# Narrow warm-up matmuls and two moved units in a fused state-space and feed-forward kernel

## The chip, the cores and the metric

The kernel runs on one core of a Trainium2 chip. The metric is the device time of one execution in microseconds (us), as the median of several runs. The engines are named as in the profile: PE is TensorE (its weight loads are listed as PEld), DVE is VectorE, ACT is ScalarE, POOL is GpSimd, SP is SyncE, which here only issues transfers.

## The reference

Two computations follow each other. The first is a chunked state-space scan over x (4 x 8 x 768 x 32), with decays a and projections B and C of width 16; the second is a bilinear feed-forward layer over its 3072 x 256 result.

```python
for c in range(nc):                       # chunks of the sequence
    cum = np.cumsum(la, axis=-1)
    L = np.exp(cum[:, :, :, None] - cum[:, :, None, :]) * causal
    CB = np.einsum('bhin,bhjn->bhij', Cc, Bc)
    y_intra = np.einsum('bhij,bhjd->bhid', CB * L, xc)
    y_inter = np.einsum('bhin,bhnd->bhid', Cc, state) * np.exp(cum)[..., None]
    y[:, :, sl] = y_intra + y_inter
    ...                                   # state = decay * state + B (x) x
x = y.transpose(0, 2, 1, 3).reshape(B * S, H * D)
a = x @ w_a                               # 256 -> 1536
b = x @ w_b
out = (a * b) @ w_out                     # 1536 -> 256
```

Inputs and outputs are float32; inside, products are taken in float16 with float32 sums.

## The kernel before

The sequence is cut into 6 blocks of 128 tokens, and the 4 batch rows into 2 pairs, which gives 12 units of work called pairs (0 to 11; pair p belongs to block p // 2). For each pair the state-space part does the following. `scale_bc` multiplies B and C by decay factors (`bm`, `cm`); a turn (`transposes` on PE for pairs 0 to 3, a transposing transfer `turn` for the later ones) gives `BT` and `CT`; `scores` takes the products of the two into the four score banks `SC`; `mask` applies the causal mask, on DVE, or, with `by_pool`, by a copy on ACT (`tmp`) and a product on POOL; `pv` or `outputs` multiplies the masked scores with `X16`, the scaled x (`scale_x`, on ACT or POOL), and adds the state's part.

The feed-forward part takes pairs 0 to 3 one by one: `unit(p, k2)` multiplies a pair with two of the twelve column tiles of Wa (`aps`) and of Wb (`bps`), ACT copies the first product out (`asb`), DVE multiplies the two (`times`, L714). `out_half` multiplies with Wo (L729). From block 2 on whole blocks are taken (`bunit`, `bout`, L759 and L784). `go((p, k2), ...)` issues whole units.

Nothing plans the order: it is written out by hand, and each engine works its instructions in program order. The result banks of PE other than `SC` are four, and the string `BANKS` says for each request in turn which of the four it gets; a request waits until the bank's last reader is done.

The start is a warm-up of PE on a tile of zeros (`warmup(n, bank, cols)`, L255), with 26 matmuls of 128 columns, then the decay scan on DVE, the factor products on PE (`factors_mm`, L283), their reciprocal on DVE (`fB`), pair 0's and pair 1's scaling, turn, scores and masks, with further warm-ups in between, mostly of 512 columns. The weights come on POOL's queue in pieces: the first half of Wa, a quarter of Wb (`load_w0`), x of pair 1, then, behind the first mask on POOL, the second quarter of Wb and the second halves.

Two later stretches matter here. After pair 1's first units the kernel issues four Wa products in a row (`us`), then their four Wb products with the multiplications, then the turn of pair 2, units (1, 4) and (1, 5), a small product `gps` and the scores of pair 2. And around pairs 4 and 5 it issues units (3, 0) to (3, 2), the scores of pair 5 with its masks and the scaling of pair 4's x on POOL (`prep_x(4)`), `out_half(2, 1)`, units (3, 3) to (3, 5), and then `group(2)`, which takes pairs 4 and 5 through `outputs` (L579, L489, L517).

Of the kernel before, what the change touches and what calls it, by code (L numbers as in the profile page):

```python
# [10 lines left out]
f32 = mybir.dt.float32  # L11
# [8 lines left out]
YS = 16.0  # L20

BANKS = (
    "01232012301230123012301230123012032103213021302132013201320132013201302310231023120130213"
    "0213023120312031203123012301230123012301230123012031203120312031203120312031203120312031"
)


# [1 line left out]
def kernel(  # L29
# [48 lines left out]
    Wb = [  # L78
        [big.tile([128, 2, KC // 2], f16, name=f"Wb0{t}") for t in range(2)],
        big.tile([128, 2, KC], f16, name="Wb1"),  # L80
    ]
# [22 lines left out]
    ffh = ctx.enter_context(tc.tile_pool(name="ffh", bufs=4))  # L104
# [7 lines left out]
    SC = [SC0[:, 0], SC0[:, 1], SC1[:, 0], SC1[:, 1]]  # L112
# [9 lines left out]
    def bank(name):  # L122
        return psf.tile([128, 512], f32, name=name, tag=f"ff{next(banks)}")
# [54 lines left out]
    def w_of(W, k, f):  # L178
        t_, q3 = W[k // 6], k % 6 // 3
        cols = t_[q3][:, f] if isinstance(t_, list) else t_[:, f, q3 * 384 : (q3 + 1) * 384]  # L180
        return cols.rearrange("p (c kk) -> p kk c", kk=3)[:, k % 3]
# [71 lines left out]
    def warmup(n, bank, cols=512):  # L253
        for _ in range(n):
            nc.tensor.matmul(  # L255
                bank[:, 0:cols], warm[:, 0:128], warm[:, 0:cols], start=True, stop=True, skip_group_check=True
            )


    def scan(lo, hi):  # L260
        for k in range(lo, hi):
            nc.vector.tensor_tensor_scan(Pr[:, k], a_sb[:, k], zero, 1.0, ALU.mult, ALU.add)
# [12 lines left out]
    def factors_mm(lo, hi, fps=None, k0=0):  # L275
        if fps is None:
            fps = bank("fps")
        w = 2 * NBP * H
        F = fps[:, k0 * w : (k0 + hi - lo) * w].rearrange("p (k r c) -> p k r c", k=hi - lo, r=2)
        for k in range(lo, hi):  # L280
            for r in range(2):
                for bt in range(2):
                    nc.tensor.matmul(  # L283
                        F[64 * bt : 64 * bt + 64, k - lo, r],
                        Pr[:, k].rearrange("p (i r) -> p r i", r=2)[:, r],
                        selr[:, k, bt],
                        start=True,
                        stop=True,
                        skip_group_check=True,
                        tile_position=(0, 64 * bt),  # L290
                    )
        return F.rearrange("p k r c -> p (k r c)")
# [14 lines left out]
    def flat(f, lo, hi):  # L307
        return f[:, lo:hi].rearrange("p k r b h -> p (k r b h)")
# [13 lines left out]
    def scale_bc(p, which, eng, factor=None):  # L322
        blk, bp = divmod(p, NBP)
        name, f = (("bm", fB), ("cm", fC))[which]
        raw = by_token(pair_in[p][which]) if p >= P0 else pair_in[p][which].rearrange("p h r n -> p r h n")
        if p >= P0 and which:
            eng.tensor_tensor(
                out=planes[p % 2][:, 4:6].rearrange("p t (h n) -> p t h n", n=N),
                in0=raw,
                in1=of_pair(f, blk, bp).unsqueeze(3).broadcast_to((128, 2, H, N)),  # L330
                op=ALU.mult,
            )
            return
        m_ = mid.tile([128, 2, H, N], f16, name=name, tag=name)
        eng.tensor_tensor(  # L335
            out=m_,
            in0=raw,
            in1=(of_pair(f, blk, bp) if factor is None else factor).unsqueeze(3).broadcast_to((128, 2, H, N)),
            op=ALU.mult,
        )  # L340
        st.setdefault(p, {})[name] = m_
        if p >= P0:
            dst = planes[p % 2][:, 0:4].rearrange("p (t e) (m f n) -> p t e m f n", e=2, f=2, n=N)
            for e in range(2):
                eng.tensor_copy(dst[:, :, e, :, e], m_.rearrange("p t (m f) n -> p t m f n", f=2)[:, :, :, e])
# [76 lines left out]
    def scores(p):  # L422
        BT, CT = st[p]["BT"], st[p]["CT"]
        st[p]["T1"] = mid.tile([128, H, 2, Q], f16, name="t1", tag="t1")
        for e, bt, m in itertools.product(range(2), range(2), range(4)) if p >= P0 else ():
            rows = slice(32 * m, 32 * m + 32)
            c0 = (e * 2 + bt) * Q
            nc.tensor.matmul(  # L428
                SC[m][:, c0 : c0 + Q],
                BT[rows, e, bt],  # L430
                CT[rows, bt],
                start=True,
                stop=True,
                skip_group_check=True,
                tile_position=(32 * m, 0),
            )
        for e in range(2) if p < P0 else ():
            for r in range(2):
                for m in range(4):
                    for bt in range(2):  # L440
                        rows = slice(32 * m, 32 * m + 32)
                        c0 = (e * 2 + r) * Q
                        nc.tensor.matmul(  # L443
                            SC[m][64 * bt : 64 * bt + 64, c0 : c0 + Q],
                            BT[rows, e, r, bt],
                            CT[rows, bt],
                            start=True,
                            stop=True,
                            skip_group_check=True,
                            tile_position=(32 * m, 64 * bt),  # L450
                        )
# [13 lines left out]
    def product0(m2, e):  # L465

        return (
            st[0]["T1"][:, 4 * m2 : 4 * m2 + 4].rearrange("p (m e) r q -> p e m (r q)", e=2)[:, e],
            (SC0, SC1)[m2][:, :, e * 256 : e * 256 + 256],
        )  # L470
# [203 lines left out]
    def unit_mm(p, k2, W, kks=range(2), ps=None):  # L674
        if ps is None:
            ps = bank("aps" if W is Wa else "bps")
        for kk in kks:
            k = 2 * k2 + kk
            for f in range(2):
                nc.tensor.matmul(  # L680
                    ps[:, kk * 2 * Q : (kk + 1) * 2 * Q],
                    w_of(W, k, f),
                    X2T[:, p, :, f],
                    start=(f == 0),
                    stop=(f == 1),
                    skip_group_check=True,
                )
        return ps
# [14 lines left out]
        return [pss[k2] for k2 in ks]  # L703

    def evac_a(a_ps, on_dve=False):
        asb = ffh.tile([128, 512], f32, name="asb", tag="asb")
        (nc.vector.tensor_copy if on_dve else nc.scalar.copy)(asb, a_ps)  # L707
        return asb

    def times(p, k2, b_ps, asb):  # L710
        s = st[p]
        if "hk" not in s:
            s["hk"] = ffh.tile([128, NK, 2 * Q], f16, name="hk", tag="hk")
        nc.vector.tensor_tensor(  # L714
            out=s["hk"][:, 2 * k2 : 2 * k2 + 2, :].rearrange("p k q -> p (k q)"), in0=b_ps, in1=asb, op=ALU.mult
        )

    def unit(p, k2, between=None):
        a_ps = unit_mm(p, k2, Wa)
        if between:  # L720
            between()
        b_ps = unit_mm(p, k2, Wb)
        asb = evac_a(a_ps)
        return lambda: times(p, k2, b_ps, asb)
# [92 lines left out]
    def go(*items):  # L817
        for p, k2 in items:
            unit(p, k2)()
# [2 lines left out]
        if ("S", p) in st:  # L822
            st[p].update(st.pop(("S", p)))

    warmup(26, SC[3], 128)
    scan(0, 1)
    over_mid(0, 1)
    sel_over_mid(0, 1, nc.vector)
# [3 lines left out]
    fps = bank("fps")  # L832
    v = factors_mm(0, 1, fps)
    nc.vector.reciprocal(flat(fB, 0, 1), v)
    warmup(1, SC[3])
    v1 = factors_mm(1, 2, bank("fps"))
    warmup(1, SC[3])
    scale_bc(0, 0, nc.vector)
    scale_bc(0, 1, nc.vector, v.rearrange("p (r b h) -> p r b h", r=2, b=NBP)[:, :, 0])
    scan(3, 4)  # L840
    tb, tcp = bank("tb"), bank("tc")
# [1 line left out]
    nc.scalar.copy(flat(fC, 0, 1), v)  # L843
    nc.scalar.copy(flat(fC, 1, 2), v1)
    scan(4, 5)
    warmup(1, SC[3])
    warmup(2, SC[3], 128)
    scores(0)
    scale_bc(1, 0, nc.gpsimd)
    mask(product0(0, 0))  # L850
# [1 line left out]
    mask(product0(1, 1), by_pool=True)  # L852
    scale_bc(1, 1, nc.vector)
    mask(product0(1, 0))
    warmup(3, tcp)
    part = transposes1(0, bank("tb"))
    part(0)
    part(1)
    warmup(2, tcp)
    py = [bank("py0"), bank("py1")]  # L860
    pv_u(0, 0, py, True)
    ds_mm(0, 256, py)
    transposes1(1, SC[0])
    for bt in range(2):
        evac0(0, bt, nc.scalar, py)
    warmup(1, tcp)
    pv_u(0, 1, py, True)
    for bt in range(2):
        evac0(1, bt, nc.scalar, py)
# [18 lines left out]
    asb = [evac_a(aps[0])]  # L888
# [35 lines left out]
        load1(nc.sync, 3, 1, bt)  # L924
    loads_x(3, nc.sync)
    loads_bc(4)
    us = [(0, 3), (0, 4), (1, 3), (0, 5)]
    asb = [evac_a(unit_mm(p, k2, Wa)) for p, k2 in us]
    for (p, k2), a_ in zip(us, asb):
        times(p, k2, unit_mm(p, k2, Wb), a_)  # L930
    transposes(2, apart=True)
    go((1, 4))
    h = unit(1, 5)
    gps = bank("gps")
    for c0 in (0, 64):
# [115 lines left out]
    prep(6)  # L1051
    masked(4, (0, 1, 2))
    out_half(2, 0)
    go((3, 0), (3, 1), (3, 2))
    scores(5)
    mask(product(5, 3), by_pool=True, by_token=True)
    prep_x(4)
# [3 lines left out]
    loads_bc(8)  # L1061
    masked(5, (0, 1, 2))
    out_half(2, 1)
    go((3, 3), (3, 4))
    scale_x(5, nc.scalar)
    go((3, 5))
    group(2)
# [92 lines left out]
```

## Time and profile before

| | us |
|---|---|
| median of 3 runs | 121.4 |
| lowest and highest run | 121.36, 122.35 |
| profiled execution, its own time | 122.31 |
| its span, from the first to the last instruction | 120.6 |
| PE busy (matmuls) | 114.6 |
| DVE, ACT, POOL busy | 87.2, 72.7, 62.3 |

The span is the part that the profile divides; the remaining 1.7 us of the execution lie around it. Busy time is a mean over stages with different limits, so it has to be read stage by stage. Times of instructions are counted from the span's start. In the lists an instruction has its start, its duration, its engine, the kernel's line, the operation, the tiles written and read, and in brackets the idle time of the engine before it with what ended it; "issue" means that nothing which the profile shows was waited for.

### The profile page before, as it was taken

The numbers are of one execution on the slowest core, as the hardware profiler recorded it, in microseconds if no ns is written. First come the engines' busy times: TensorE is split into PE (matmuls) and PEld (weight loads), VectorE is DVE, ScalarE is ACT, GpSimd is POOL, SyncE is SP. The second block draws the span as 40 slices with busy tenths as digits, with TensorE's granted clock in tenths as the row PEclk, the third lists the DMA queues.
The fourth block names the chain that finished last, engine by engine and source line by source line (L and its number), as shares of the span: only waits on it lengthen the run. The fifth ranks groups of instructions, "written<-read, shape, count | busy, mean of one in ns | idle before, by whom it ended". The sixth has DMA issues, their size and how long they took to land.

```text
span 120.6 us, 3713 instructions
## 1 busy us (share of the span) xinstructions
PE 114.6 (95%) x1454; PEld 80.5 (67%) x1454; DVE 87.2 (72%) x171; ACT 72.7 (60%) x148; POOL 62.3 (52%) x109
## 2 busy tenths in 40 slices
PE   5998699999999999999999999999999999999990
PEld 5745499888898898645476464766464684655890
DVE  5989695995989888499984999677899445847100
ACT  0477557685965767787667737645646737566220
POOL 6998998299985686199912992249200000000200
PEclk9999999999999999999999999999999999999999
DMA  3999999997879999699588954879301012010032
GB/s 62 128 173 163 177 208 168 236 159 72 82 107 94 151 112 143 111 131 159 56 147 121 247 184 98 88 109 192 134 0 49 2 43 85 0 49 0 20 110 87
DMA packets 69185, 13.44 MB, mean 111 GB/s; under 512 B 64048, under 2 KB 68912, under 8 KB 69168
## 3 DMA queue, kind: packets, MB, share of 16 engines
q1 hardware_dynamic: 62272, 9.31, 47.5%
q0 software_dynamic: 4368, 3.54, 18.2%
q10 hardware_dynamic: 2528, 0.36, 2.1%
q8 instruction: 11, 0.18, 0.6%
q14 instruction: 6, 0.05, 0.1%
HBM read 11.11 MB, written 3.15 MB: 118 GB/s over the span
## 4 chain that ended last, share of the span: by engine, by line
PE 93%; DVE 3%; issue 1%; ACT 0%
PE ops L784 18%; PE aps L759 18%; PE bps L759 17%; PE ops L729 9%; PE bps L680 9%; PE aps L680 8%; PE SC L255 3%; PE SC L428 2%; PE SC L489 2%; PE SC L443 1%; DVE t L483 1%; PE SC L503 1%; PE aps L695 1%; PE SC L579 1%; PE fps L283 1%
## 5 line engine op out<-in xcount | busy, mean ns | idle before, releaser
L707 ACT COPY asb<-aps 128x512 f32<-128x512 f32 x72 | 41.6, 587 | 13.3 <-PE aps L759 9.6
L769 DVE TENSOR_TENSOR hkb<-bps,asb 128x512 f16<-128x512 f32 x48 | 32.3, 689 | 12.7 <-ACT asb L707 11.6
L759 PE MATMUL aps<-XB,Wa 128*128 128x512 f16 x96 | 28.6, 379 | 0.0
L759 PE MATMUL bps<-XB,Wb 128*128 128x512 f16 x96 | 28.5, 379 | 0.0
L784 PE MATMUL ops<-Wo,hkb 128*128 128x256 f16 (+1 forms) x204 | 22.5, 267 | 0.0
L784 PEld LDWEIGHTS <-hkb 128*128 128x128 f16 x204 | 18.5, 98 | 3.1
L483 DVE TENSOR_TENSOR t<-SC,causal_q 128x512 f16<-128x512 f32 x27 | 17.2, 682 | 3.3 <-PE SC L428 3.3
L714 DVE TENSOR_TENSOR hk<-bps,asb 128x512 f16<-128x512 f32 x24 | 16.1, 684 | 3.1 <-PE bps L680 1.2
L759 PEld LDWEIGHTS <-Wb 128*128 128x128 f16 x96 | 9.9, 103 | 10.9
L759 PEld LDWEIGHTS <-Wa 128*128 128x128 f16 x96 | 9.7, 103 | 9.1 <-issue 0.2
L798 POOL DMA_DIRECT2D out_dram<-osb x1 | 0.6, 642 | 27.9 <-ACT osb L796 27.9
L796 ACT ACTIVATE osb<-ops 128x256 f32<-128x256 f32 (+1 forms) x16 | 6.0, 377 | 14.3 <-PE ops L784 14.2
L680 PE MATMUL bps<-X2T,Wb 128*128 128x256 f16 x96 | 13.8, 273 | 0.0
L680 PE MATMUL aps<-X2T,Wa 128*128 128x256 f16 x88 | 12.7, 273 | 0.0
L729 PE MATMUL ops<-Wo,hk 128*128 128x256 f16 x96 | 11.5, 273 | 0.0
L481 POOL TENSOR_TENSOR t<-tmp,causal_q 128x512 f16<-128x512 f32 x5 | 5.8, 1159 | 10.0 <-ACT tmp L480 9.9
L680 PEld LDWEIGHTS <-Wb 128*128 128x128 f16 x96 | 9.8, 103 | 0.7
L729 PEld LDWEIGHTS <-hk 128*128 128x128 f16 x96 | 8.9, 98 | 1.4
L680 PEld LDWEIGHTS <-Wa 128*128 128x128 f16 x88 | 8.9, 103 | 0.6
L320 POOL TENSOR_SCALAR x<-xn 128x512 f16<-128x512 f32 x6 | 8.9, 1491 | 0.6
L483 DVE TENSOR_TENSOR t<-SC,causal 128x512 f16<-128x512 f32 x12 | 7.7, 683 | 0.8 <-PE SC L443 0.7
L335 POOL TENSOR_TENSOR bm<-bn,fB 128x256 f16<-128x256 f32 x11 | 6.9, 623 | 2.5 <-DMA bn<-in_B_dram 2.3
(115 smaller groups left out, 127.8 us busy)
## 6 DMA issues: line engine op xcount, KB each, us to landing
out_dram<-osb SPq DMA_DIRECT2D x22, 128.0 KB, 1.8
xn<-in_x_dram SPq DMA_DIRECT2D x6, 256.0 KB, 4.3
cn<-in_C_dram SPq DMA_DIRECT2D x8, 128.0 KB, 3.9
bn<-in_B_dram SPq DMA_DIRECT2D x8, 128.0 KB, 4.5
Wa<-in_moe_w_a_dram POOLq DMA_DIRECT2D x2, 384.0 KB, 6.4
Wo<-in_moe_w_out_dram POOLq DMA_DIRECT2D x2, 384.0 KB, 5.5
xn<-in_x_dram SPq DMA_DIRECT2D x4, 128.0 KB, 3.7
Wb<-in_moe_w_b_dram POOLq DMA_DIRECT2D x2, 192.0 KB, 6.1
```

The lines of the kernel that those rows point to most:

```text
L320: eng.tensor_scalar(xo, xi, XS, None, ALU.mult)
L335: eng.tensor_tensor(out=m_, in0=raw, in1=(of_pair(f, blk, bp) if factor is None else factor).unsqueeze(3).broadcast_to((128, 2, H, N)), op ...
L481: nc.gpsimd.tensor_tensor(out=o_, in0=tmp, in1=c_, op=ALU.mult)
L483: nc.vector.tensor_tensor(out=o_, in0=i_, in1=c_, op=ALU.mult)
L680: nc.tensor.matmul(ps[:, kk * 2 * Q : (kk + 1) * 2 * Q], w_of(W, k, f), X2T[:, p, :, f], start=(f == 0), stop=(f == 1), skip_group_check=True,
L707: (nc.vector.tensor_copy if on_dve else nc.scalar.copy)(asb, a_ps)
L714: nc.vector.tensor_tensor(out=s["hk"][:, 2 * k2 : 2 * k2 + 2, :].rearrange("p k q -> p (k q)"), in0=b_ps, in1=asb, op=ALU.mult)
L729: nc.tensor.matmul(o_ps[:, 0:d_model], hk[:, k, bt * Q : (bt + 1) * Q], Wo[:, k, :], start=(k == 0), stop=(k == NK - 1), skip_group_check= ...
L759: nc.tensor.matmul(t_, w_of(W, k, f), XB[:, blk - P0 // NBP, f].rearrange("p t j q -> p (t j q)"), start=(f == 0), stop=(f == 1), skip_gro ...
L769: return lambda: nc.vector.tensor_tensor(out=s["hk"][:, k], in0=ps[1], in1=asb, op=ALU.mult)
L784: nc.tensor.matmul(o_ps[:, 0:w], hk[:, k, c * Q : (c + 1) * Q], Wo[:, k, cs], start=(k == 0), stop=(k == NK - 1), skip_group_check=True,)
L796: nc.scalar.activation(out=o_sb[:, 0:w], in_=o_ps[:, 0:w], func=AF.Copy, scale=1.0 / (YS * YS))
```

## The change

The change does four things. Warm-ups of 512 columns become four times as many of 128 columns, and the first group grows from 26 to 34 matmuls. In the stretch after pair 1's units five Wa products are taken in a row instead of four (the fifth is that of unit (1, 4)), and the turn of pair 2 now stands between the two products of that unit; the buffers of `asb` go from four to six. Unit (3, 3) moves ahead of the scores of pair 5. The bank string is written anew to go with the new order.

```diff
 BANKS = (
-    "01232012301230123012301230123012032103213021302132013201320132013201302310231023120130213"
-    "0213023120312031203123012301230123012301230123012031203120312031203120312031203120312031"
+    "01232012301230123012301230123012023102312031203123012301230123012301203210321032130120312"
+    "0312032130213021302132013201320132013201320132013021302130213021302130213021302130213021"
 )
...
-        asb = ffh.tile([128, 512], f32, name="asb", tag="asb")
+        asb = ffh.tile([128, 512], f32, name="asb", tag="asb", bufs=6)
...
-    warmup(26, SC[3], 128)
+    warmup(34, SC[3], 128)
     scan(0, 1)
...
     v = factors_mm(0, 1, fps)
     nc.vector.reciprocal(flat(fB, 0, 1), v)
-    warmup(1, SC[3])
+    warmup(4, SC[3], 128)
     v1 = factors_mm(1, 2, bank("fps"))
-    warmup(1, SC[3])
+    warmup(4, SC[3], 128)
...
     scan(4, 5)
-    warmup(1, SC[3])
-    warmup(2, SC[3], 128)
+    warmup(6, SC[3], 128)
     scores(0)
...
-    warmup(3, tcp)
+    warmup(12, tcp, 128)
     part = transposes1(0, bank("tb"))
     part(0)
     part(1)
-    warmup(2, tcp)
+    warmup(8, tcp, 128)
     py = [bank("py0"), bank("py1")]
...
-    warmup(1, tcp)
+    warmup(4, tcp, 128)
     pv_u(0, 1, py, True)
...
-    us = [(0, 3), (0, 4), (1, 3), (0, 5)]
+    us = [(0, 3), (0, 4), (1, 3), (0, 5), (1, 4)]
     asb = [evac_a(unit_mm(p, k2, Wa)) for p, k2 in us]
-    for (p, k2), a_ in zip(us, asb):
+    for (p, k2), a_ in zip(us[:4], asb):
         times(p, k2, unit_mm(p, k2, Wb), a_)
     transposes(2, apart=True)
-    go((1, 4))
+    times(1, 4, unit_mm(1, 4, Wb), asb[4])
     h = unit(1, 5)
...
     out_half(2, 0)
-    go((3, 0), (3, 1), (3, 2))
+    go((3, 0), (3, 1), (3, 2), (3, 3))
     scores(5)
...
     out_half(2, 1)
-    go((3, 3), (3, 4))
+    go((3, 4))
     scale_x(5, nc.scalar)
     go((3, 5))
     group(2)
```

## The prediction

> **What bounds the kernel now.** I read the busy table first, then a table by stage, then the chain that ended last, and only after that single places in the timeline.
>
> ```profile
> PE 114.6 (95%) x1454; PEld 80.5 (67%) x1454; DVE 87.2 (72%) x171; ACT 72.7 (60%) x148; POOL 62.3 (52%) x109
> ```
>
> A mean of 95% says little about where PE (TensorE) is free. The busy time of each engine by stage does (us, then PE, PEld, DVE, ACT, POOL busy with counts, granted clock, DMA share, GB/s):
>
> ```profile
> 11.00:14.76 3.76, 2.68 (x66) 2.09 (x66) 2.59 (x6) 2.36 (x8) 3.19 (x7) 1.00 1.23 171
> 14.76:40.00 25.24, 25.24 (x395) 22.55 (x395) 20.84 (x42) 18.08 (x39) 20.52 (x38) 1.00 0.96 139
> 40.00:80.00 40.00, 40.00 (x509) 25.06 (x508) 32.16 (x60) 27.83 (x52) 23.30 (x37) 1.00 0.82 132
> ```
>
> From 14.76 us on PE is busy in every microsecond; the trace lists no wait of a matmul after that. So the end is the moment at which this dense stretch begins, plus its fixed work, plus any stall that the change puts into it. Time can be won only before 14.76, and lost anywhere. What sets 14.76 is in the chain that ended last (start, us, what):
>
> ```profile
> 1.25 2.95 PE SC L255 x26
> 4.21 0.54 PE fps L283 x8
> ...
> 12.41 0.66 PE bps L680 x6
> 13.06 0.34 PE SC L503 x30
> 13.40 1.08 issue
> 14.48 0.21 PE SC L503
> 14.69 0.08 PE SC L530 x14
> 14.77 0.83 PE bps L680 x6
> ```
>
> PE stands 1.08 us in the middle of pair 1's product of scores and x (L503), waiting for nothing that has a name. By then 222 matmuls and 227 weight loads have begun. The transfers of 12 to 13 us show a candidate, a single packet on queue 8:
>
> ```profile
> q0 software_dynamic: 205, 0.17, 128.5%
> q8 instruction: 1, 0.02, 6.0%
> ```
>
> Queue 8 carries 11 packets in the whole span, for 2908 PE instructions, about 264 for a packet. I read the stop as PE waiting for its next block of code, in a stretch where the DMA engines are full. A second bound lies beside it. The products that come next use the Wb piece that POOL issues at 9.21 us; it lands 5.5 us later, at 14.7. Both bounds end within 0.05 us of each other, so removing one wins nothing.
>
> **The change, part by part.** *More and narrower warm-ups.* Wide ones (512 columns) become four narrow ones (128). At full clock two wide ones take 0.59 us and a single one 0.379, so 0.21 us each. The group of one wide and two narrow at 6.12 us lasts 0.49; less the last one's 0.219 and 0.21, a narrow one takes 0.055 to 0.06. Four narrow cost 0.22 to 0.24, nothing to speak of against one wide. Only the first group really grows, 26 to 34. There the clock is still low: 26 in 2.95 us, one lasting 0.311, so 0.106 each, and eight more are 0.85 us. If the TensorE clock rises meanwhile it is 8 x 0.055 = 0.44 us. I take 0.85, since the wide warm-up at 4.68 us still took 0.61 us.
>
> This delays something real. PE works in order, and the factor products (L283) start at 4.13, right behind warm-up 26, though their operand (selr) was ready at 3.72. They move to about 5.0. Part of them then runs at the higher clock, seen in before from about 5.3 us, which gives 0.04 back: about 0.8 us for DVE's reciprocal at 4.79, and with it pair 0's factors, scores and masks, and pair 1's masks, which end at 12.93 and feed L503 at 12.99. L503 would start at 13.80. It takes 0.2 us before the stop and 0.28 after it (14.48 to 14.76), so PE would be ready for the Wb piece at about 14.24. That is 0.5 us before it lands.
>
> Does the piece land later? POOL issues it behind the mask at 8.11 us, which waits for the same chain, so the issue moves from 9.21 to 10.0. But queue 0 was full all that time (share over 100% in the rows above), and pair 1's x, issued on it earlier, lands only at 12.7. The piece waits behind it either way: landing 14.7, cost 0. The cover is 0.5 us on PE and some 2 us on POOL; without the first the loss is what exceeds it. POOL's later issues (pair 2's inputs, Wo) move by 0.8 too; their landings, 18.9 us and on, lie behind the second weight halves on the same queue. Pair 2's cm, 20.90 now, is ready by 21.3; the turn that uses it moves to 22.0.
>
> *Five Wa products in a row.* PE's work is the same in another order. The four Wb products start one product (0.437 us, the spacing of four 256-column matmuls in the chain) later, and DVE's multiplications with them. DVE and ACT between 20 and 24.4 us (start, us, engine, line):
>
> ```profile
> 20.51 2.48 DVE L714 TENSOR_TENSOR hk<-bps,asb 128x512 f16<-128x512 f32 x4 [1.18 <-PE bps L680]
> 22.91 0.44 DVE L382 COPY ct<-SC 128x256 f16<-128x256 f16 x1
> 23.32 0.69 DVE L714 TENSOR_TENSOR hk<-bps,asb 128x512 f16<-128x512 f32 x1
> 24.34 0.69 DVE L483 TENSOR_TENSOR t<-SC,causal 128x512 f16<-128x512 f32 x1 [0.33 <-PE SC L443]
> ```
>
> The copy of pair 2's ct stands behind the four multiplications. It starts at 23.35 instead of 22.91 and ends at 23.79, and the scores of pair 2 need it. PE reaches them at 23.64 as before. They start 0.055 us after the copy (as in the earlier pairs), at 23.84: a stall of **0.20 us**. Bounds: 0, if DVE's first multiplication starts as early as now, and 0.44, if PE had reached the scores when ct ends in before. Queued behind the scores are the output products (L729); DVE's masks follow 0.2 later and are not waited for. I followed the new bank string through this stretch. The fifth Wa product takes the bank whose copy ends at 19.28, at 19.81. The small G product takes the one that DVE frees at 23.44, at 23.61. No bank is late; a bank late by more than these covers would cost its excess. The six asb buffers add no work.
>
> *Unit (3,3) ahead of pair 5's scores.* The scores start a unit, 0.874 us, later (41.44 to 42.31). What follows them, on ACT, POOL and PE:
>
> ```profile
> 41.96 0.59 ACT L480 COPY tmp<-SC 128x512 f32<-128x512 f32 x1 [0.27 <-PE SC L428]
> 42.63 1.16 POOL L481 TENSOR_TENSOR t<-tmp,causal_q 128x512 f16<-128x512 f32 x1 [1.46 <-ACT tmp L480]
> 43.88 1.50 POOL L320 TENSOR_SCALAR x<-xn 128x512 f16<-128x512 f32 x1
> 45.46 0.63 POOL L327 TENSOR_TENSOR planes<-cn,fC 128x256 f16<-128x256 f32 x1
> 46.05 0.63 PE L489 MATMUL SC<-t,x 128*32 128x128 f16 x32
> ```
>
> POOL waits for ACT's tmp, masks, and only then scales pair 4's x, which L489 reads. That x ends at 45.38 now, 0.67 before its use; 0.874 later it ends at 46.25 and L489 starts at 46.31: a stall of **0.26 us**. Bounds: 0, if POOL is faster without DVE beside it, and 0.87. SP's turn of pair 7 waits for POOL's planes, whose bm already waits 0.56 us for a load: it moves by about 0.3 us from 47.89, for scores at 54.26. SP's loads behind it move as much and have over 2 us.
>
> **The sum.** Start 0, scores 0.20, x 0.26: +0.46 us. The profiled execution took 122.31 us, 120.6 of it span and 1.7 around it; the sum gives a span of 121.1. The median of the runs is 121.4, 0.9 below that execution, and I set the sum on the median: 121.4 + 0.46 = **121.9 us**.
>
> **Rivals.** *1, slower: the code stop moves ahead of the Wb products.* The change adds 35 matmuls and their weight loads, 70 instructions, all ahead of this place. A stop at the 449th instruction then falls 70 earlier in the program, at the six products of 12.24 us (379 had begun by 12.28). The request for the block goes out earlier too: one block before the stop is L503 of pair 0 at 8.73 now, pair 0's scores at about 7.6 then. From request to release is 5.75 us now, which would give a release at 13.35 and a stop of 0.3, hidden. But if the full queue decides and the release stays at 14.48, then six products (0.66), a switch (0.09), L503 (0.2) and the rest (0.28) come behind it: dense start 15.70, +0.94, in all +1.40: 122.8 us. It decides once the release comes after 13.55. For it: the packet ran in a full queue. Against: the request is 1.1 us earlier.
>
> The Trainium skill, page "Runtime: NRT & Kernel Launch", section "Instruction fetch mechanics", says that code is refilled in 16 KiB blocks of 256 instructions and that crossing a boundary is mostly hidden. The packet size agrees (0.18 MB in 11 packets); that it is hidden does not agree with a 1.08 us stop, if I read the stop rightly. By that rule rival 1 falls away and the sum stays +0.46.
>
> *2, the start comes earlier.* If the Wb piece lands sooner than in the profiled execution, the old kernel still stood until 14.48 for code, and the new one goes dense at 14.24: -0.52, in all -0.06: 121.3 us. Against: queue 0 is full and in order.
>
> *3, the median run has neither late code nor a late piece.* Then its 0.9 us come from a dense start at about 13.85, and the new chain (14.24) is late by 0.4: +0.85: 122.3 us. For it: the size of that 0.9; against: nothing else shows it.
>
> **How the numbers follow.** Forecast 0.38, rival 1 0.26, rival 2 0.17, rival 3 0.14, none of these 0.05. One per cent, 1.2 us, is about what a measurement of this kernel can tell from no change. Slower by over 1% is rival 1 and a tail of rival 3 (0.02): 0.28. Faster by over 1% would need a dense start before 13.1, a tail of rival 2 (0.05) and of the rest (0.02): 0.07. Within 1%: 0.65. The range goes from 121.0, below rival 2, to 122.9, over rival 1; the likeliest case alone, by the bounds of its two stalls, spans 121.4 to 122.7.
>
> **What would show it.** Right: the factor products near 5.0 us, no stop in L503 but a wait for the Wb piece until about 14.7, pair 2's scores at 23.8 behind ct, L489 near 46.5 behind POOL's x. Rival 1 shows as a stop before 14.5 us ahead of the first bps products, and a dense start past 15. The prediction is wrong if the dense stretch begins more than 0.3 us from 14.76, or if a stall appears in it that I have not named.

## The result and the profile after

The changed kernel takes 123.38 us (median of 21 runs, 122.48 to 124.36) against 122.43 us for the kernel before on the same chip (21 runs, 121.36 to 123.71). The ratio is 1.0087, interval [1.0063, 1.0112], so about 1 us more: within 1%, on the slow side. The median of before is itself 1 us above the 121.4 of its first three runs, so it is the difference that has to be compared: +0.46 us was forecast, +0.95 (medians) to +1.07 (ratio) was measured. A ratio leaves out the runs that lie more than 1.5% above the fastest of their kernel, a median here does not; the table below gives both.

The profiled execution took 123.42 us, 121.7 of it span, 1.1 more than the one of before. Its busy line and stages, in the columns of the prediction:

```profile
PE 115.8 (95%) x1489; PEld 82.7 (68%) x1489; DVE 87.3 (72%) x171; ACT 72.7 (60%) x148; POOL 62.3 (51%) x109
```

```profile
11.00:14.61 3.61, 3.41 (x114) 2.75 (x115) 3.24 (x7) 2.77 (x8) 3.05 (x7) 1.00 1.08 137
14.61:40.00 25.39, 24.70 (x396) 21.69 (x388) 20.08 (x42) 17.34 (x38) 20.69 (x37) 1.00 0.90 137
40.00:80.00 40.00, 39.82 (x496) 25.27 (x494) 32.08 (x60) 27.73 (x52) 23.56 (x38) 1.00 0.87 136
```

The share of PE is 95% as before and says nothing. The stages do: the dense stretch begins 0.15 us earlier (14.61), and then it has holes, 0.69 us up to 40 us and 0.18 behind it, where before had none. Both profiled executions lie within 0.15 us of the median of their kernel, and in this pair the loss lies behind the start. Four views show where.

The start, from the chain that ended last (start, us, what):

```profile
13.35 0.12 issue
13.47 0.71 PE bps L680 x5
14.17 0.35 PE SC L503 x32
14.52 0.16 PE SC L530 x16
```

The stop of 1.08 us inside L503 is gone; what is left of it is a short one ahead of the second of the six Wb products (13.47). L503 runs through, and the dense products follow at PE's own pace, though the Wb piece had landed at 14.05.

The turn of pair 2 and its scores, from the timeline:

```profile
22.15 0.11 PEld L357 LDWEIGHTS <-cm 128*128 128x128 f16 x2 [0.21 <-POOL cm L335]
...
23.19 0.43 DVE L382 COPY ct<-SC 128x256 f16<-128x256 f16 x1
...
23.68 0.19 PEld L935 LDWEIGHTS gps<-hsx,c 32*64 32x64 f32 x4 [0.21 <-DVE ct L382]
```

PE waits 0.21 us for POOL's cm, which the prediction had ready by 21.3; it is ready at 22.09. The later wait for ct then costs nothing more: from the unit's last Wb product to the first output product it is 0.70 us here as in before.

The third hole is the largest, 0.77 us in L503 of pair 3 at 35.76. The chain that ended last leads back from it, through POOL, to a load, and from the load to SP's queue:

```profile
21.49 0.45 SPq L143
...
26.97 4.97 DMA cn<-in_C_dram
...
32.08 0.39 POOL planes L327
...
34.59 1.13 POOL t L481
...
35.76 0.27 PE SC L503 x9
```

SP issues the loads of pairs 3 and 4 in order (L143, L160), and the first of them waits until the second half of Wb has landed: 19.89 us here, 18.69 in before. So pair 4's cn is issued at 26.97 instead of 24.71 and lands at 31.94 instead of 28.48 (1.2 us of this is that wait; the two issues of x between took 4.15 us instead of 3.07); POOL, which scales pair 4 ahead of pair 3's fourth mask (`mask(product(3, 3), by_pool=True)`) in its program, stands 1.27 us for it, and its mask starts at 34.55 instead of 32.88. In before the chain of these microseconds names PE alone.

The fourth is L489:

```profile
45.58 1.50 POOL L320 TENSOR_SCALAR x<-xn 128x512 f16<-128x512 f32 x1
...
47.14 0.35 PE L489 MATMUL SC<-t,x 128*32 128x128 f16 x12 [0.18 <-POOL x L320]
```

L579 stands at 46.64 here, and L489 follows 0.50 us after it, waiting for x; the same step took 0.25 us less in before. Forecast were 0.26.

### The profile page after: what moved, and what is told of

It is laid out like the page before. It is cut to its first block, busy times and chain, and to the rows that moved or that the text cites. A ratio compares the mean times of both kernels' runs of the same rounds, so it can differ in the third digit from the quotient of the medians.

```text
span 121.7 us, 3784 instructions
## 1 busy us (share of the span) xinstructions
PE 115.8 (95%) x1489; PEld 82.7 (68%) x1489; DVE 87.3 (72%) x171; ACT 72.7 (60%) x148; POOL 62.3 (51%) x109
## 4 chain that ended last, share of the span: by engine, by line
PE 74%; POOL 7%; SPq 4%; DMA 4%; issue 4%; DVE 3%; ACT 1%; POOLq 0%; ACTq 0%; DVEq 0%
PE ops L784 18%; PE aps L759 17%; PE bps L759 17%; SPq L143 4%; DMA cn<-in_C_dram 4%; PE aps L680 4%; PE SC L255 4%; PE bps L680 3%; POOL t L481 3%; PE ops L729 2%; PE SC L428 2%; PE SC L489 2%; POOL x L320 1%; DVE t L483 1%; POOL bm L335 1%
## 5 line engine op out<-in xcount | busy, mean ns | idle before, releaser
L680 PE MATMUL bps<-X2T,Wb 128*128 128x256 f16 x96 | 13.9, 273 | 0.1
L680 PE MATMUL aps<-X2T,Wa 128*128 128x256 f16 x88 | 12.6, 273 | 0.0
L680 PEld LDWEIGHTS <-Wb 128*128 128x128 f16 x96 | 9.7, 103 | 0.9 <-issue 0.3
L680 PEld LDWEIGHTS <-Wa 128*128 128x128 f16 x88 | 8.9, 103 | 0.6
L327 POOL TENSOR_TENSOR planes<-cn,fC 128x256 f16<-128x256 f32 x8 | 5.0, 622 | 8.6 <-DMA cn<-in_C_dram 7.3
```

What stands on the lines that cost most here:

```text
L327: eng.tensor_tensor(out=planes[p % 2][:, 4:6].rearrange("p t (h n) -> p t h n", n=N), in0=raw, in1=of_pair(f, blk, bp).unsqueeze(3).broadc ...
L680: nc.tensor.matmul(ps[:, kk * 2 * Q : (kk + 1) * 2 * Q], w_of(W, k, f), X2T[:, p, :, f], start=(f == 0), stop=(f == 1), skip_group_check=True,
```

## The experiments

Eighteen kernels, each in five rounds beside the kernel before on the same chip. Three columns are from the one profiled execution of each: start of L503 of pair 1 (PE is ready for the Wb piece about 0.5 us later where nothing stops it), start of the dense stretch, and the stops behind that start of 0.2 us or more, with their place. A stop is what lies between two starts on PE beyond the same step in a kernel that does not wait there; the idle time in the brackets of a view comes out 0.07 to 0.17 us shorter.

| kernel | medians, us | ratio | L503 | dense | stops |
|---|---|---|---|---|---|
| before | | | 12.99 | 14.76 | none |
| after | +0.95 | 1.0087 [1.0063, 1.0112] | 14.10 | 14.61 | 0.21 turn, 0.77 L503, 0.25 L489 |
| e1: all but 34 | +0.52 | 1.0054 [1.0023, 1.0085] | 13.22 | 15.38 | 0.21 L503, 0.25 L489 |
| e2: only 34 | +0.54 | 1.0032 [0.9997, 1.0067] | 13.78 | 14.33 | 0.46 turn, 0.36 scores of pair 6 |
| e3: only unit (3,3) | -0.13 | 0.9985 [0.9949, 1.0022] | 13.76 | 14.51 | 0.25 L489 |
| e4: only five | -0.02 | 0.9981 [0.9947, 1.0015] | 14.05 | 14.89 | 0.45 scores of pair 6 |
| e5: after, Wb piece first | +0.58 | 1.0070 [1.0041, 1.0099] | 14.63 | 15.13 | 0.25 L489 |
| e6: before, Wb piece first | +0.31 | 1.0022 [0.9988, 1.0056] | 13.59 | 14.10 | 0.95 Wb products at 20.1, 0.33 turn |
| e7: narrow, 26 | -0.02 | 0.9969 [0.9927, 1.0012] | 13.14 | 13.69 | 0.70 L503, 0.33 scores of pair 6 |
| e8: after, mask first | +2.40 | 1.0194 [1.0137, 1.0251] | 14.26 | 14.77 | 1.96 scores of pair 4, 0.25 L489 |
| e9: both moves | +0.44 | 1.0000 [0.9958, 1.0042] | 13.76 | 14.97 | 0.25 L489 |
| e10: warm-ups | +0.76 | 1.0075 [1.0034, 1.0115] | 14.62 | 15.59 | 0.46 L503 |
| e11: first group 50 | +1.16 | 1.0109 [1.0061, 1.0157] | 14.36 | 14.87 | 0.20 turn, 0.44 scores of pair 5, 0.62 of pair 6 |
| e12: first group 18 | +0.22 | 1.0003 [0.9961, 1.0045] | 13.40 | 14.32 | none |
| e13: after, SP free | +0.45 | 1.0040 [1.0006, 1.0075] | 14.03 | 14.53 | 0.25 L489 |
| e14: before, SP free | -0.31 | 0.9971 [0.9939, 1.0003] | 13.76 | 14.27 | 0.45 and 0.46 turn |
| e15: warm-ups, SP free | +0.05 | 1.0006 [0.9971, 1.0041] | 14.34 | 14.85 | none |
| e16: after, 18, SP free | -0.08 | 1.0016 [0.9982, 1.0049] | 13.73 | 14.23 | 0.25 L489 |
| e17: five, SP free | -0.34 | 0.9982 [0.9947, 1.0018] | 13.84 | 15.24 | 0.76 scores of pair 6 |
| e18: five, 18, SP free | +0.03 | 1.0005 [0.9973, 1.0037] | 13.76 | 14.63 | 1.13 scores of pair 6 |

One profile is one execution, and the executions of one kernel spread over 1 us and more, mostly about 2. So the times decide what an edit costs, and the profiles only by which way.

**The change in its parts.** e1 puts the first group back to 26:

```diff
-    warmup(34, SC[3], 128)
+    warmup(26, SC[3], 128)
```

> The whole change, but the first group of warm-ups stays at 26. Theory A (the eight added warm-ups delay POOL's weight loads; queue 0 runs thin, the second half of Wb lands 1.2 us later, with it pair 4's cm, and POOL, waiting for it, masks pair 3 late): factor products near 4.13 us, second half of Wb by 18.9, no wait of L503 for POOL near 35 us; what is left are the waits of the two moved units, +0.2 and +0.25, together +0.45 us, ratio 1.004. Rival B (the late landing comes from the narrow form or from the new order, not from the eight): the wait near 35 us of about 0.8 us stays and the time is +1.0 us, ratio 1.008.

e2 is the kernel before with that group alone at 34:

```diff
-    warmup(26, SC[3], 128)
+    warmup(34, SC[3], 128)
```

> Only the first group grows from 26 to 34; the wide warm-ups and the order of before stay. Theory A: POOL's issue of the second Wb quarter moves from 9.21 to about 10.0 us, the second half of Wb lands at 19.5 us or later, L503 of pair 3 waits 0.5 to 0.8 us for POOL's mask, +0.6 us (0.4 to 0.9), ratio 1.005. Rival B: landing as before, +0.1 us or less, ratio 1.000 to 1.001.

e3 is the kernel before with unit (3,3) alone moved ahead of `scores(5)`:

```diff
-    go((3, 0), (3, 1), (3, 2))
+    go((3, 0), (3, 1), (3, 2), (3, 3))
     scores(5)
...
-    go((3, 3), (3, 4))
+    go((3, 4))
```

> Only unit (3, 3) moves ahead of pair 5's scores; the bank string of before serves both orders. Predicted: L489 near 46 us waits for POOL's x of pair 4, 0.26 us, and the time is +0.26 us, ratio 1.002. Rival (the wait exists only where POOL is already late from pair 4's loads): no wait, 0.

e4 is the kernel before with the five Wa products, the later turn, the six buffers and the new bank string:

```diff
-    us = [(0, 3), (0, 4), (1, 3), (0, 5)]
+    us = [(0, 3), (0, 4), (1, 3), (0, 5), (1, 4)]
...
     transposes(2, apart=True)
-    go((1, 4))
+    times(1, 4, unit_mm(1, 4, Wb), asb[4])
```

> Only five Wa products in a row, the turn of pair 2 inside unit (1, 4), six buffers, and the bank string of after. Predicted: DVE's copy of ct ends near 23.8 us and pair 2's scores start 0.2 us late, +0.2 us, ratio 1.0016. Rival (the 0.2 us of after was POOL's late cm alone, at the turn): the turn does not wait, scores at 23.64 to 23.7, +0 us.

Measured: eight further warm-ups alone cost about half of the loss (e2, its interval just touching 1); either move alone costs nothing that shows (e3, e4, with intervals up to +0.3 and +0.2 us); the changed kernel without the eight still costs about half (e1). The two halves add up to the whole. The profile of e1 tells little of its half: its start waited 1.59 us for the Wb piece, which was issued at 9.14 us, as in before, and landed at 15.34. In e2 the second half of Wb landed at 18.88, nearly as early as in before, so the way over that piece, which after shows, isn't the only one by which the eight cost; PE there waited 0.46 us at the turn of pair 2 for POOL's cm, ready at 21.78 instead of 20.90. That e3 is free has a likely reason in its profile: L489 does stop 0.25 us, but where the unit is not moved, the scores of pair 6 (L428, about 50 us) often wait 0.33 to 0.45 us for their turn (e2, e4, e7), and with the move they don't. One stall takes the other's place.

The stall behind ct that was forecast for the five products stands in e4's profile, just under the limit of the table, and more plainly in e13, one of the kernels further below:

```profile
23.12 0.43 DVE L382 COPY ct<-SC 128x256 f16<-128x256 f16 x1
...
23.70 0.43 PE L443 MATMUL SC<-ct,bt 32*64 32x128 f16 x32
```

The scores start 0.15 us after ct ends, and 0.31 after the small product ahead of them, in before 0.02. The output products follow the unit's last Wb product by 0.88 us instead of 0.70, so PE loses 0.18. Nine of the ten profiles with the five products show it (e1, e4, e5, e8, e9, e13, e16, e17, e18); in the tenth, after's, the wait for cm comes first.

**Issue the Wb piece earlier.** e5 (on after) and e6 (on before) move its issue ahead of the mask that waits for the factor chain:

```diff
+    load_w0(1, 1)
     mask(product0(1, 1), by_pool=True)
...
-    load_w0(1, 1)
     w1 = load_w(1)
```

> The changed kernel, with POOL's issue of the second Wb quarter taken from behind the first mask on POOL to ahead of it (between pair 1's bm and that mask, where POOL stood idle for 0.98 us). Theory C (the added warm-ups delay PE's start, PE's start delays POOL's mask, the mask delays the issue of the weights to 10.0 us, and queue 0 runs thin between 11 and 12.5 us; what follows on that queue, on SP and on POOL is then late and stops PE at pair 2's turn, in L503 of pair 3 or at a later turn): issue near 8.0 us, queue 0 has moved over 1220 KB by 14 us (1133 in the changed kernel, 1274 in before), the stops between 20 and 50 us shrink from 1.2 to about 0.5, time -0.5 us against the changed kernel, so about +0.4 against before, ratio 1.003. Rival D (those stops come from PE running in a new order, not from the loads): time as the changed kernel, ratio 1.008.

> Before, with the same one move of POOL's issue. Theory C: when the TensorE clock rises late, before has the same thin queue (issue 9.98 us in two profiles with 26 warm-ups), so the earlier issue helps it in part of its executions: -0.2 to -0.5 us, ratio 0.996 to 0.998. Rival D: 0. The mask on POOL ends about 0.7 us later, at 9.95, and is needed at 10.2.

Measured: it brings nothing on before, and on after 0.2 (ratios) to 0.4 us (medians), with overlapping intervals. In e5 the piece landed at 13.60 and the dense stretch began at 15.13 all the same: there PE's own chain was the late one (L503 at 14.63), so the landing of the piece is not what held that start. In e6 the start came at 14.10, and 0.95 us of it went back at 20.1 us to products that waited for the second half of Wb. For before the expectation was a gain, so theory C failed there.

**Narrow alone, and the mask first.** e7 is the kernel before with every warm-up made narrow as in the change, and the first group left at 26:

```diff
     warmup(26, SC[3], 128)
...
-    warmup(3, tcp)
+    warmup(12, tcp, 128)
...
```

> Before, with all warm-ups narrow and the first group at 26: the narrow form alone. Predicted: nothing to 0.05 us for PE. Theory C: it leaves POOL's issue where the clock puts it, so 0, ratio 1.000 (0.998 to 1.002). Rival E (the 54 instructions more move PE's code blocks to places where PE has no cover, or the narrow form costs PE time): +0.3 us or more, ratio 1.003.

e8 changes POOL's order in after, so that pair 3's fourth mask doesn't stand behind pair 4's load:

```diff
-    prep(4, (2,))
     mask(product(3, 3), by_pool=True)
+    prep(4, (2,))
```

> The changed kernel, with pair 3's mask on POOL ahead of pair 4's scaling there, so that it no longer waits for pair 4's loads. Theory C: the stop of 0.8 us in L503 of pair 3 goes; pair 4's turn starts up to 1.2 us later than in the changed kernel and may hold its scores near 37.9 us for 0.3: together -0.4 us against the changed kernel, ratio to before 1.005. If the stop was a chance of the one profile: 0 to +0.3 against the changed kernel, ratio 1.009 to 1.011.

Measured: narrow warm-ups are free (e7). Its profile has a stop of 0.70 us in L503 of pair 3 all the same, though the second half of Wb had landed at 18.29: PE came there at 33.62, 1.1 us ahead of after, and POOL's mask ended at 34.50. So with an early start PE runs into POOL's mask as well, and that stop alone doesn't show what the eight cost. e8 was expected to win 0.4 us on after and loses 2.4 us on before: the stop in L503 goes, but the turn of pair 4 is now issued at 35.29 and landed at 39.16, and pair 4's scores wait 1.96 us for it. The load that came late held POOL in the one order and holds the turn in the other. The table by stage of e8 shows a second loss behind that stop (granted clock third from the right):

```profile
36.00:39.16 3.16, 1.31 (x13) 0.98 (x10) 1.97 (x5) 1.26 (x3) 2.38 (x6) 1.00 0.93 92
...
40.10:43.40 3.30, 3.30 (x18) 2.31 (x16) 1.43 (x3) 1.06 (x3) 2.83 (x5) 0.52 0.85 122
```

Behind a stop of 2 us, in a stretch where PE was busy less than half the time, the granted clock is 0.52 for 3.3 us, which by an estimate (0.48 of 3.3) costs some 1.6 us more. That belongs to the profiled execution (126.37 us, mean clock 0.986) alone: in the other five, 124.75 to 125.55 us, the mean clock is 0.999 or 1.00, so the 2.4 us of the median are not made by it.

**Both moves, and the warm-ups whole.** e9 has the edits of e3 and e4 together, with wide warm-ups and a first group of 26. e10 has those of e2 and e7 together, so the warm-ups of after and the order of before.

> The kernel before with both moves and nothing else: five Wa products in a row with the turn of pair 2 inside the unit, and unit (3,3) ahead of pair 5's scores; the warm-ups stay wide and the first group stays 26. Theory 1: each move alone cost nothing only because the wait of pair 6's scores at about 50 us (0.36 to 0.45 us where unit (3,3) is not moved) took its place; both together lose the two stalls that the prediction summed, 0.1 to 0.2 us at the turn or the scores of pair 2 and 0.25 us at L489, so +0.3 to +0.6 us, with 0.25 us ahead of L489 in the profile and no wait at pair 6's scores. Rival: the moves don't add up, and what the whole change loses lies in the warm-ups: -0.1 to +0.2 us.

> The other half: all warm-ups narrow with a first group of 34, the order of the kernel before. Theory 1: narrow costs nothing (0 with a first group of 26), eight more cost 0.4 to 0.5 us as they did with wide warm-ups (+0.3%), so +0.4 to +0.5 us. Rival, in which nearly the whole loss of the change lies in the warm-ups (a start that is late whenever 34 meets a late rise of the clock): +0.8 to +1.1 us. In the profile: L503 of pair 1 at 13.8 to 14.3 us with an early rise of the clock, 14.6 with a late one.

Measured: the warm-ups carry most of the loss, +0.76 us. For the moves the median says +0.44 and the ratio 0, with half a microsecond of interval to both sides. e9's profile has the 0.25 us at L489 and no wait of pair 6's scores, as its first theory said, and the 0.18 at pair 2's scores; the cost of the moves was left open here.

**The dose.** e11 has a first group of 50 and e12 one of 18, in the kernel before:

```diff
-    warmup(26, SC[3], 128)
+    warmup(50, SC[3], 128)     # e11; e12: 18
```

> The kernel before with a first group of 50 instead of 26, nothing else: a dose. Theory 1 (PE works in order, so every warm-up beyond the readiness of selr at 3.72 us delays the factor products): 24 more at 0.106 us are +2.5 us at low clock, some 1.5 to 1.9 with the clock rising meanwhile; L503 of pair 1 at 14.5 to 15.5 us, the dense stretch begins at 15.0 to 16.0, +1.0 to +2.0 us. Rival (the Wb piece and the second weight halves decide, and move little): at most +0.5 us.

> The kernel before with a first group of 18, nothing else. By theory 1 the factor products then start with selr at about 3.78 us instead of 4.13, 0.35 us earlier at PE; the Wb piece is issued as much earlier. If PE's chain decides in most executions: -0.2 to -0.35 us. If the landing of the Wb piece decides: 0. If fewer warm-ups make the clock rise in its later place more often (it cost 0.8 us at L503 where it was seen): +0.2 to +0.8 us, with the rise at 9 to 11 us in the profile.

Measured: 50 cost 1.16 us, 18 nothing. The size for 50 was as expected by theory 1, the place only in part: its dense stretch begins at 14.87, just before the range given, and 1.26 us of stops follow. The profiles show what sets PE's readiness. The factor products (L283) of before, and below them the second eight of e9, which starts with the same instructions, with its stop in L503, from the timelines of PE (e9's first eight are as in before):

```profile
4.13 0.61 PE L283 MATMUL fps<-selr,Pr 32*64 32x16 f32 x8
5.21 0.44 PE L283 MATMUL fps<-selr,Pr 32*64 32x16 f32 x8
```

```profile
5.21 0.61 PE L283 MATMUL fps<-selr,Pr 32*64 32x16 f32 x8
...
14.75 0.23 PE L503 MATMUL SC<-t,x 64*32 64x128 f16 x2 [0.58 <-issue]
```

Eight of them take 0.61 us as long as TensorE is not at full speed, 0.41 to 0.44 once it is. In before the durations fall at about 5.3 us, in e9 at about 9 us; in after, whose products start at 4.99, at about 6. The trace's own records of the granted clock begin at 5.31, 8.91 and 5.99 us, the same places; the profile counts the time ahead of the first record as 1.00. L503 of pair 1 follows: with 26 it starts at 12.99 to 13.59 where the rise was early (before, e1, e6, e7) and at 13.76 to 14.05 where it was late (e3, e4, e9, e14, e17); with 34 at 13.78 to 14.34 early (after, e2, e8, e13, e15) and at 14.62 and 14.63 late (e5, e10). By the means of these groups eight warm-ups put L503 0.8 to 0.9 us later and a late rise 0.5 to 0.6, and they add up; in four of the five early ones with 34 the short stop of 0.3 to 0.6 us ahead of L503 is part of it. The three profiles with 18 (13.40 to 13.76) all have the late rise, of nine with 26 five, of seven with 34 two. That more warm-ups make an early rise likelier is suggested by this and not shown.

The Trainium skill, page "TensorE: Matmul & The Clock Gate", Part 1, says that the clock rises after a sustained window of about 3.4 us that runs freely and does not start with the kernel. The trace agrees on the window: its clock records last 3.413 us or whole multiples of it (but for the last of each trace, which the end cuts off), and the rises of before and e9 lie 3.6 us apart. In the twenty profiles the rise is at 4.2 to 6.0 or at 8.9 to 10.2 us, never between. The same page, section "Why this matters for your kernels", sets the fall at gaps of more than about 3 us; in e8 a stop of 2 us was enough.

**Take SP's wait away.** The common node of the late second chain is the second half of Wb. SP's loads are held behind it on purpose; now they are held behind the second half of Wa, which lands 2 to 3 us earlier ("SP free" below and in the table):

```diff
-    tc.add_manual_dep(b3[0].ins, w1[1].ins.name, ...)
+    tc.add_manual_dep(b3[0].ins, w1[0].ins.name, ...)
```

e13 does this in after, e14 in before, e15 in e10's kernel, e16 in after with a first group of 18.

> The changed kernel, with SP's loads of pair 3's inputs waiting for the second half of Wa (landed at 17.1 us) instead of that of Wb (19.9), nothing else. Theory A (the later warm-ups cost through the second chain: POOL's issues, second half of Wb, SP's loads, POOL's scaling): the stop of L503 of pair 3 at 35.8 (0.77 us in the changed kernel) goes, SP's loads start at about 17 us, and 0.4 to 0.8 us come back: +0.2 to +0.6 us over the kernel before. Theory B (the loss is at the dense start, where PE's own chain or the Wb piece is late): the start is as before, nothing comes back: +0.8 to +1.1 us. Against both: the earlier loads take rate from the second half of Wb and its products wait for it at about 20 us: over +1.1 us.

> The same edit on the kernel before: SP's loads wait for the second half of Wa (16.6 us) instead of Wb (18.7). Its profile shows no stop after the dense start, so by both theories little to win: -0.3 to 0 us, unless the median execution has the stops of 0.4 to 0.7 us that single changes showed at 35 and 50 us (then -0.3 to -0.6). If the second half of Wb then lands after its first use at about 20.3 us: +0.3 us or more.

> The warm-ups half (all narrow, first group 34, order of before) with the same edit of SP's loads. It cost +0.76 us without the edit, with a stop of 0.46 us at L503 of pair 3 (36.2 us) and a dense start at 15.6 us. Theory A: 0.3 to 0.5 us come back, +0.2 to +0.5 us. Theory B: nothing comes back, +0.6 to +0.9 us.

> The whole change with a first group of 18 and the same edit of SP's loads: both suspected costs of the larger group are taken away. What is left is the order's: 0.2 to 0.5 us of stalls at the turn of pair 2 and at L489. Theory A and B together: +0.1 to +0.5 us. If it comes out below the kernel before (-0.2 us or less), it is a version that beats both. Rival (narrow warm-ups themselves cost): +0.6 us or more.

Measured: 0.5 us come back in after and 0.7 in the warm-ups half, and the stop at 35 us goes from 0.77 to nothing and from 0.46 to below 0.1. The chain of e13 at this place, where after's led through POOL and SP:

```profile
34.49 0.22 PE SC L547 x4
34.72 0.35 PE SC L503 x32
```

But the control moves too: before gains 0.31 us by the same edit (interval up to 1.0003), so its median execution seems to lose something there as well, though its profile shows no stop. With SP free in all, the differences are: warm-ups (e15 less e14) +0.36 us, the two moves on top (e13 less e15) +0.40, a first group of 18 instead of 34 (e16 less e13) -0.54 (-0.29 by the ratios). Of after's 0.95 the moves would then take about 0.4, the warm-ups some 0.35 off SP's chain, and what is left, 0.2, is what the eight make worse on it. Each of these carries 0.4 to 0.5 us of uncertainty to both sides, so how they rank is not settled, and that the 0.35 arises at the start is argued, not shown. Best shown is that a longer first group still costs with SP free: e13 and e16 differ in that alone, on the same chip, 12 runs each, by 123.05 to 122.51 us.

**A version from the parts.** e17 has the edits of e14 and e4 in the kernel before, e18 those and a first group of 18 (e12).

> A version put together from the runs: the kernel before with SP's loads of pair 3 waiting for the second half of Wa (that edit alone: -0.31 us, with 0.90 us of stops at the turn of pair 2 in its profile, at 21.5 and 22.1, where PE waits for POOL's bm and cm) and with the five Wa products and the later turn (alone: 0), which gives POOL's bm and cm of pair 2 about 0.7 us more. If those stops are what the first edit loses, both together: -0.4 to -0.8 us, with at most 0.3 us of stops at the turn. Rival (the dense start decides, the stops of one execution are not those of the median one): -0.3 to 0 us.

> The same with a first group of 18 warm-ups. The whole change with 18 and the same wait of SP came out at -0.08 us with 0.25 us of stop at L489, which the move of unit (3,3) makes; without that move, by the sum, -0.3 us; with the factor products 0.35 us earlier, if the start is not held by the Wb piece, -0.4 to -0.8 us. Rival (fewer warm-ups let the clock rise late more often, which cost 0.8 us at L503): no better than with 26, -0.3 to +0.2 us.

Measured: -0.34 and 0 us, both intervals across 1, so neither reaches the 0.4 us expected. The stops at the turn of pair 2 that e14 showed are gone from both profiles, and a wait of 0.76 and 1.13 us for the turn of pair 6 (50.9 us) stands in their place; both profiles are of long executions (123.76 and 123.60 us), so the median one may wait less. No version here is shown to beat the kernel before; e14 (122.28 us) comes nearest, its interval reaching 1.0003.

## Why the prediction was wrong, point by point

**The two stalls of the moves were right.** L489 was forecast 0.26 us late behind POOL's x: 0.25, in every profiled kernel with unit (3,3) moved. Pair 2's scores were forecast 0.20 late behind ct: 0.18, in the nine kernels with the five products other than after. In after's profile 0.21 us at the turn, for cm, stand in its place. Together 0.46 was forecast, and e13 against e15 gives +0.40, though with an uncertainty as large. Alone neither cost anything that shows, probably because the wait of pair 6's scores gives way; the prediction had no such term.

**The code stop behaved as read.** It was expected to shrink with the request going out earlier, and it shrank to 0.3 us inside the six Wb products, as rival 1's own first branch said (release at 13.35, a stop of 0.3). Rival 1 itself, a release that stays at 14.48, did not come. The stop stands at the same count in every profile that has one: 449 matmuls and weight loads have begun ahead of it, in L503 for before, e3 and e9, in L680 for after, e8, e13 and e15, in L530 for e12. The constant count in kernels with different instructions speaks for code; nothing here shows the fetch itself. Twelve of the twenty profiles have no such stop. What the prediction didn't know is how much its length scatters: 1.08 us in before, 0.58 in e9, under 0.1 in e3 with the same start of the program.

**The step that failed is "Start 0".** It put the warm-ups' term of the sum at nothing. Together they measured +0.76 us (e10), which with the moves' 0 to 0.4 is the whole loss; the narrow form costs nothing (e7), the eight alone 0.4 to 0.5 (e2). The term stood on two claims.

The first was a cover of 0.5 us on PE: L503 at 13.80, ready at 14.24, the Wb piece at 14.7. After had L503 at 14.10, and with a late rise of the clock it is 14.6 (e5, e10), so the cover is gone in some executions. That after's profiled start, 14.61, lies near the forecast 14.76 is luck: the piece came 0.65 us earlier and PE 0.37 later than reckoned. In e5 the dense stretch then began at 15.13, though the piece had landed at 13.60; in e10 PE was ready at 15.0, and the piece, issued at 10.84 by the same late chain, landed at 15.54. Over all profiles the cover did much of its work: L503 starts at 13.57 in the mean of nine with 26 and at 14.25 in that of seven with 34, the dense stretch at 14.65 and 14.83. Single starts scatter by some 1.5 us, so how much the start lost stays open.

The second claim was that POOL's issues, 0.8 us later, cost nothing, since "queue 0 was full all that time" and the later landings "lie behind the second weight halves". For the Wb piece itself that held: issued at 9.0 to 9.2 us it landed at 14.57 in the mean of three, issued at 9.95 to 10.04 at 14.46 in the mean of ten. For what follows it, POOL's own timeline refutes it. After:

```profile
10.04 0.76 POOL L176 DMA_DIRECT2D Wb<-in_moe_w_b_dram  x1
...
11.49 0.72 POOL L168 DMA_DIRECT2D Wb<-in_moe_w_b_dram  x1
...
20.18 0.70 POOL L143 DMA_DIRECT2D xn<-in_x_dram  x1 [0.74 <-DMA Wb<-in_moe_w_b_dram]
20.89 0.64 POOL L335 TENSOR_TENSOR bm<-bn,fB 128x256 f16<-128x256 f32 x1
21.47 0.62 POOL L335 TENSOR_TENSOR cm<-cn,fC 128x256 f16<-128x256 f32 x1
```

In before the same lines stand at 9.21, 10.66, 18.97 (after a wait of 0.35), 19.68 and 20.27, and from 7.4 to 21.5 us POOL is never free but for that wait and one of 0.4 us at 11.4. An engine almost without a gap passes a delay on: so all its issues came 0.83 us later, and then it waited for the second half of Wb, which landed 1.2 us later: cm of pair 2 comes 1.2 us late and not 0.4, and SP's loads, held behind the same piece, as much. The way over POOL is no chance of one profile: where the clock rose early, cm is ready at 20.90 in the mean with 26 (before, e1, e7) and at 21.66 with 34 (after, e2, e8, e13, e15). On SP's way the 0.77 us in L503 of pair 3 followed, a stall that the prediction had not named. The queue was not full either: from 11.0 to 12.3 us it took 527 packets and 0.20 MB in before, 371 and 0.09 MB in after.

```profile
q0 software_dynamic: 527, 0.20, 137.8%
```

```profile
q0 software_dynamic: 371, 0.09, 83.5%
```

A share above 100% had been read as a queue with work always waiting, on which a later issue costs nothing; with the later issue the queue ran at half the bytes. How much of the 1.2 us is the late issue and how much is scatter stays open. In the profiles the second half of Wb, issued at 10.5 to 10.7 us, landed at 18.7 in the mean of three (before, e1, e7); issued at 11.4 to 11.6, at 19.0 in the mean of eleven, from 17.8 (e5) to 19.9; issued at 12.0 and 12.3, at 19.7 and 20.0 (e11, e10).

**The rivals.** Rival 2 needed a start at 14.24; 14.61 came, for L503 was 0.3 later than reckoned. Rival 3 has the size (+0.85) and the right engine in after's profile, where PE's own chain is the late one. Its reason, a dense start of before at 13.85 in most executions, is not what the profiles show: those with a first group of 26 begin at 13.69 to 15.38. The 0.9 us themselves were a chance of three runs.

**The base.** The forecast 121.9 us and the measured 123.38 differ by 1.5 us, of which 1.0 is no loss of the change: the sum was set on 121.4, the median of three runs, and 21 runs of the same kernel give 122.43. The profiled execution (122.31), taken for a slow one, was an ordinary one.

## What to carry to other kernels

Before an edit on an early engine is costed at nothing, look at the engine that issues the transfers: if it has no gap between the edit and the next use, the delay arrives at everything behind it, on other queues too where they are held behind one of its pieces. A cover read from one profile is one draw; where the start of an execution scatters by more than the cover, some executions don't have it. And a stall found in one profile is worth its length only if no other chain is nearly as late: here one of 0.25 us cost nothing that shows while another wait stood behind it.

## What the runs showed of the hardware

- PE's stop, which I read as one for code, comes after the same 449 instructions in all eight profiles that show it (twelve show none), and lasts from under 0.1 to 1.08 us. The Trainium skill, page "Runtime: NRT & Kernel Launch", section "Instruction fetch mechanics", calls the crossing of a block mostly hidden; in before and in e9 it was not.
- TensorE came to full speed at 4.2 to 6.0 us or at 8.9 to 10.2 us. Both occur with the same first instructions (before 5.31, e9 8.91). The granted clock of a profile reads 1.00 from the start in both, because the time ahead of the trace's first clock record counts as full; the durations tell the difference.
- A stop of 1.96 us in e8 was followed by one window of 3.41 us at half the clock, which began 0.7 us after PE went on.
